# Three evictions of the steady unit in another order on ScalarE: a cross-network kernel bound by TensorE

## The chip, the cores and the metric

The kernel runs on one core of one Trainium2 chip. The metric is device time in microseconds, the median over several executions. Before the change it was 2277.09 us (three runs, 2276.94 to 2277.36).

## The reference, cut to what matters

```python
B, Din, L = 16384, 1024, 6          # bf16
x = x0
for l in range(L):
    proj = einsum('bd,de->be', x, ws[l]) + bs[l]
    x = x0 * proj + x
```

Six layers, each a 16384 x 1024 by 1024 x 1024 product, a bias, a product with x0 and a sum.

## The kernel before

The batch is cut into 16 blocks of 1024 rows. A block in one layer is a **unit**; there are 96. In a unit the product is done with seven half-size products in place of eight (P1 to P7, sums and differences of the operands are made by VectorE as T1 to T4, those of the weights are stored ahead). Two of the seven, 5 and 2, are cut once more in the same way into seven **inner products** (5p1 to 5p7, 2p1 to 2p7). So TensorE does 20 groups of four 512-wide matmuls and 14 groups of four 256-wide ones a unit.

Partial sums live in eight PSUM banks, A0 to A3 and X0 to X3. ScalarE empties them. It does three kinds of work: evictions with the bias (E1.m, E3.m, E7.m, E4.m), evictions of inner results (5e_..., 2e_...: c11, c12 and c21 are quadrants of the result, u3 an intermediate sum), and **forks** (5f1, 5f2, 2f1, 2f2, F.m): copies of a partial sum from one bank to another, so that two sums can go on from it. Each fork and eviction frees or fills a bank that a following matmul group waits for.

The order of all work is not written as a loop. Each operation has a rank, a planned time in us within the unit, and the program is emitted in order of rank as far as dependencies allow. Every engine then does its own list strictly in that order. One table, R2, is used by 87 units: all but the first eight, which have tables of their own, and the last.

```python
R2 = ranks("""
P1.0@0 P1.2@0.86 5p5@1.73 5p1@2.16 P1.3@2.6 2p1@3.46 5p2@3.9 5p6@4.34 2p5@4.78 P1.1@5.21 5p7@6.08 5p3@6.51 2p2@6.95
2p6@7.39 5p4@7.82 P6.0@8.26 P6.1@9.13 2p7@9.99 2p3@10.43 P3.0@10.86 2p4@11.73 P6.2@12.16 P3.1@13.03 P6.3@13.89
P3.2@14.75 P3.3@15.62 P7.1@16.48 ...
E1.0@1.07 5e_p5@2.38 5f1@3.03 E1.2@3.48 5e_c11@4.55 5f2@5.2 2e_p5@5.65 2f1@6.3 5e_u3@6.75 E1.3@7.23 E1.1@7.8
2e_c11@8.37 5e_c21@8.85 2f2@9.33 F.0@9.78 5e_c12@10.23 2e_u3@10.71 2e_c12@11.18 F.1@11.66 E3.0@12.11 2e_c21@12.68
F.2@13.23 E3.1@14.1 F.3@14.96 E3.2@15.82 E3.3@16.69 ...
T1@-1.14 5t13@0.59 5t2@3.06 2t13@3.39 5t4@5.13 2t2@6.6 T2@6.93 2t4@8.07 T4@8.4 5cc@10.88 T3@11.48 2cc@12.61 Q1@13.35
Qm@14.62 Qa@15.89 Ua@17.43 ...
""")
```

The inner products and their evictions (X is "5" with banks a, b = 0, 1, or "2" with banks 2, 3):

```python
inner(5, b, True)
copy(X + "e_p5", ip5[X][:], v3(b), ...)
inner(1, a, True)
copy(X + "f1", pX[b][:], pX[a][:], ...)      # first fork: bank a into bank b
inner(2, b, False)
copy(X + "e_c11", c(0, 0), v3(b), ...)
inner(6, a, False)
copy(X + "f2", pX[b][:], pX[a][:], ...)      # second fork
inner(3, b, False)
copy(X + "e_c12", iu[X][:, 0], v3(b), ...)
inner(7, a, False)                           # 2p7: bank X2 must have been forked
copy(X + "e_u3", iu[X][:, 1], v3(a), ...)
inner(4, a, False)                           # 2p4: bank X2 must have been read
copy(X + "e_c21", c(1, 0), v3(a), ...)
ttop(X + "cc", ...)                          # VectorE: needs c12, u3 and p5
...
for m in range(KH):                          # after the inner products
    xb = m if one else m % 2                 # steady units fork into X0 and X1
    group(f"P6.{m}", "6", pA[m], ...)        # P6.1 needs A1 evicted by E1.1; P6.0 needs T2
    copy(f"F.{m}", pX[xb][:], pA[m][:], ...)
    group(f"P3.{m}", "3", pX[xb], ...)
    biased(f"E3.{m}", U[:, m, :], pX[xb][:], ...)
```

Of the kernel before, what the change touches and what calls it, by code (L numbers as in the profile page):

```python
# [26 lines left out]
P1.0@0 P1.2@0.86 5p5@1.73 5p1@2.16 P1.3@2.6 2p1@3.46 5p2@3.9 5p6@4.34 2p5@4.78 P1.1@5.21 5p7@6.08 5p3@6.51 2p2@6.95  # L27
2p6@7.39 5p4@7.82 P6.0@8.26 P6.1@9.13 2p7@9.99 2p3@10.43 P3.0@10.86 2p4@11.73 P6.2@12.16 P3.1@13.03 P6.3@13.89
P3.2@14.75 P3.3@15.62 P7.1@16.48 P7.0@17.34 P7.2@18.21 P7.3@19.07 P4.1@19.93 P4.0@20.8 P4.2@21.66 P4.3@22.52
E1.0@1.07 5e_p5@2.38 5f1@3.03 E1.2@3.48 5e_c11@4.55 5f2@5.2 2e_p5@5.65 2f1@6.3 5e_u3@6.75 E1.3@7.23 E1.1@7.8  # L30
2e_c11@8.37 5e_c21@8.85 2f2@9.33 F.0@9.78 5e_c12@10.23 2e_u3@10.71 2e_c12@11.18 F.1@11.66 E3.0@12.11 2e_c21@12.68
F.2@13.23 E3.1@14.1 F.3@14.96 E3.2@15.82 E3.3@16.69 E7.0@18.41 E7.1@18.98 E7.2@19.55 E7.3@20.14 E4.0@21.87 E4.1@22.44
E4.2@23.01 E4.3@23.59
T1@-1.14 5t13@0.59 5t2@3.06 2t13@3.39 5t4@5.13 2t2@6.6 T2@6.93 2t4@8.07 T4@8.4 5cc@10.88 T3@11.48 2cc@12.61 Q1@13.35
Qm@14.62 Qa@15.89 Ua@17.43 Um@18.7 Ux@19.97 Va@21.11 Wma@23.38 Wmb@24.58 Wx@25.31 Vm@27.38 Vx@28.85
# [609 lines left out]
```

## Time and profile before

| | before |
|---|---|
| time, median | 2277.09 us |
| span of the profiled run | 2275.3 us |
| steady unit, from 2p7 to 2p7, median | 23.451 us |
| stall of TensorE ahead of 2p7, median | 0.065 us in 81 of 87 units (0.089 in three more) |
| stall of TensorE ahead of P3.3, median | 0.012 us in all 87 units |
| VectorE busy / ScalarE busy | 92% / 81% |

The stalls are read from the trace instruction by instruction: a 512-wide matmul is followed by the next start after 0.216 us, a 256-wide one after 0.109 us, and what goes beyond that is a stall; stalls of 0.003 us and more are counted. The list of waits counts otherwise: its entry of 84 waits and 15.4 us, in the prediction, holds the idle time of weight loads, and 0.118 us of each (0.216 less the 0.098 that a load takes) is the ordinary pause between two loads. 84 x (0.118 + 0.065) is 15.4. The busy share of TensorE is of no use for this, since the recorded matmuls overlap and cover gaps of this size. The lines themselves stand in the prediction.

### The profile page before, as it was taken

What the parts mean: (1) busy time and instruction counts of PE and PEld (TensorE: products, weight loads), DVE (VectorE), ACT (ScalarE), POOL (GpSimd) and SP (SyncE); (2) the same over time, 40 slices, a digit from 0 to 9 for tenths busy, and PEclk for the clock granted to TensorE, in tenths of its full rate; (3) what the DMA queues carried; (4) which work ended last, traced back from release to release, by engine and by line L of the source; (5) the groups of instructions that cost most, each with busy time, mean ns of one, the idle gap of its engine ahead of it and who ended that gap; (6) DMA issues with size and microseconds to landing.
All of it is one profiled execution on the core that took longest, in us unless ns stands there. A gap on an engine that the chain in (4) does not pass through costs nothing.

```text
span 2275.3 us, 35076 instructions
## 1 busy us (share of the span) xinstructions
PE 2267.7 (100%) x12993; PEld 1266.7 (56%) x12993; DVE 2084.0 (92%) x2331; ACT 1844.5 (81%) x3234; POOL 24.5 (1%) x46
## 2 busy tenths in 40 slices
PE   9999999999999999999999999999999999999998
PEld 4455555555555555555555555555555555555554
DVE  8999999999999999999999999999999999989997
ACT  6678888888888888888888888888888888888887
POOL 1110000000000000000000000000000000000000
PEclk9999999999999999999999999999999999999999
DMA  8779797796977969779697796977969689696872
GB/s 280 231 269 297 252 249 262 221 297 210 246 264 222 286 216 255 257 220 286 213 269 247 227 283 205 283 235 227 286 200 286 232 230 286 196 291 227 234 248 66
DMA packets 620493, 557.03 MB, mean 245 GB/s; under 512 B 391456, under 2 KB 546592, under 8 KB 620320
## 3 DMA queue, kind: packets, MB, share of 16 engines
q1 hardware_dynamic: 614240, 534.58, 79.0%
q0 software_dynamic: 5488, 19.93, 2.3%
q8 instruction: 102, 1.67, 0.3%
q14 instruction: 71, 0.58, 0.1%
q10 hardware_dynamic: 592, 0.27, 0.0%
HBM read 437.79 MB, written 52.43 MB: 215 GB/s over the span
## 4 chain that ended last, share of the span: by engine, by line
PE 99%; DMA 0%; ACT 0%; DVE 0%; issue 0%
PE pA L289 58%; PE pX L411 24%; PE pX L289 17%; DMA ev<-in_x_dram 0%; PE pX L359 0%; PE pA L505 0%; PE pX L505 0%; DVE x0T L516 0%; ACT x0T L363 0%; ACT pX L294 0%; PE pA L366 0%
## 5 line engine op out<-in xcount | busy, mean ns | idle before, releaser
L289 PEld LDWEIGHTS <-wp 128*128 128x128 bf16 x7904 | 772.5, 98 | 839.5 <-issue 1.6
L289 PE MATMUL pA<-T,wp 128*128 128x512 bf16 x4608 | 1055.1, 379 | 0.0
L298 ACT ACTIVATE ev<-pA,b_all 128x512 bf16<-128x512 f32 x1123 | 705.0, 691 | 211.2 <-PE pA L289 210.8
L411 PEld LDWEIGHTS <-wp 128*128 128x128 bf16 x4984 | 487.0, 98 | 157.3 <-issue 15.4
L202 DVE TENSOR_TENSOR ev<-ev,x0T 128x2048 bf16<-128x2048 bf16 (+2 forms) x483 | 482.9, 1002 | 8.1 <-ACT ev L298 1.5
L202 DVE TENSOR_TENSOR xst<-ev,xst 128x2048 bf16<-128x2048 bf16 x319 | 389.1, 1220 | 19.1 <-DVE ev L202 0.9
L411 PE MATMUL pX<-ti,wp 128*128 128x256 bf16 x2848 | 397.6, 272 | 0.0
L202 DVE TENSOR_TENSOR ev<-ev,ev 128x2048 bf16<-128x2048 bf16 (+1 forms) x283 | 343.9, 1215 | 25.7 <-ACT ev L298 7.6
L289 PE MATMUL pX<-xst,wp 128*128 128x512 bf16 x1376 | 336.3, 379 | 0.0
L298 ACT ACTIVATE ev<-pX,b_all 128x512 bf16<-128x512 f32 x412 | 289.4, 706 | 56.1 <-PE pX L289 46.5
L289 PE MATMUL pA<-xst,wp 128*128 128x512 bf16 x1280 | 313.5, 379 | 0.0
L294 ACT COPY pX<-pA 128x512 f32<-128x512 f32 x412 | 256.2, 625 | 39.1 <-PE pA L289 38.4
L294 ACT CAST ev<-pX 128x512 bf16<-128x512 f32 x384 | 225.2, 620 | 47.8 <-ACT ev L298 37.3
L202 DVE TENSOR_TENSOR ev<-iu,ip 128x1024 bf16<-128x1024 bf16 x178 | 122.6, 689 | 121.1 <-ACT iu L294 121.1
L294 ACT COPY pX<-pX 128x512 f32<-128x512 f32 x356 | 208.7, 587 | 8.7 <-ACT ev L294 0.2
L294 ACT CAST iu<-pX 128x512 bf16<-128x512 f32 x356 | 197.0, 640 | 0.0
L202 DVE TENSOR_TENSOR T<-xst 128x2048 bf16<-128x2048 bf16 x160 | 194.9, 1218 | 0.3
L202 DVE TENSOR_TENSOR T<-xst,T 128x2048 bf16<-128x2048 bf16 x160 | 195.0, 1219 | 0.2
L411 PE MATMUL pX<-T,wp 128*128 128x256 bf16 x1068 | 160.2, 273 | 0.0
L294 ACT CAST ip<-pX 128x512 bf16<-128x512 f32 x178 | 104.8, 589 | 54.0 <-PE pX L411 54.0
L411 PE MATMUL pX<-xst,wp 128*128 128x256 bf16 x888 | 133.2, 273 | 0.0
L202 DVE TENSOR_TENSOR xst<-ev,x0T 128x2048 bf16<-128x2048 bf16 x64 | 78.3, 1223 | 1.6
(50 smaller groups left out, 641.0 us busy)
## 6 DMA issues: line engine op xcount, KB each, us to landing
wp<-Lc SPq DMA_DIRECT2D x538, 512.0 KB, 4.6
wp<-in_ws_dram SPq DMA_DIRECT2D x287, 512.0 KB, 5.4
out_dram<-x0T SPq DMA_DIRECT2D x30, 1024.0 KB, 8.7
Lc<-wp POOLq DMA_DIRECT2D x24, 512.0 KB, 5.9
Lc<-isum POOLq DMA_DIRECT2D x12, 512.0 KB, 6.7
w<-in_ws_dram SPq DMA_DIRECT2D x5, 512.0 KB, 6.3
ev<-in_x_dram SPq DMA_DIRECT2D x3, 512.0 KB, 7.0
out_dram<-x0T SPq DMA_DIRECT2D x3, 256.0 KB, 3.9
```

The costliest lines, as they stand in the source:

```text
L202: nc.vector.tensor_tensor(out=o, in0=a, in1=b, op=op)
L289: nc.tensor.matmul(bank[:], lhsT=wt[(u, w)][:, k, m * P:(m + 1) * P], rhs=rhs[:, k, :], start=(start and k == 0), stop=(k == KH - 1), skip ...
L294: add(name, lambda: nc.scalar.copy(out=dst, in_=src), rd, wr)
L298: add(name, lambda: nc.scalar.activation(out=dst, in_=src, func=IDENT, bias=b_all[:, c:c + 1], scale=1.0), rd, wr)
L411: nc.tensor.matmul(pX[bank][:, m * NQ:(m + 1) * NQ], lhsT=wv[:, k, m * P:(m + 1) * P], rhs=rhs[:, k, :], start=(start and m == 0 and k == ...
```

## The change

Its intent is to get the second fork of inner product 2 (2f2) done earlier, so that 2p7 finds its bank ready. To make room, 2e_c11, which frees the bank that 2f2 writes, goes ahead of the eviction of bank A1 (E1.1), 5e_c21 goes behind the fork, and 2e_c21 goes ahead of E3.0. Only ranks change, and only ScalarE's list comes out different; the lists of TensorE, VectorE, GpSimd and SyncE are the same.

```diff
-E1.0@1.07 ... 5e_u3@6.75 E1.3@7.23 E1.1@7.8
-2e_c11@8.37 5e_c21@8.85 2f2@9.33 F.0@9.78 5e_c12@10.23 2e_u3@10.71 2e_c12@11.18 F.1@11.66 E3.0@12.11 2e_c21@12.68
-F.2@13.23 E3.1@14.1 ...
+E1.0@1.07 ... 5e_u3@6.75 E1.3@7.23 2e_c11@7.8 E1.1@8.28
+2f2@8.85 5e_c21@9.33 F.0@9.81 5e_c12@10.43 2e_u3@10.9 2e_c12@11.38 F.1@11.86 2e_c21@12.37 E3.0@12.85
+F.2@13.45 E3.1@14.1 ...
```

(Cuts marked with "...".)

More of the change, by code (lines that the diff above doesn't have):

```diff
@@ L29 @@
 P3.2@14.75 P3.3@15.62 P7.1@16.48 P7.0@17.34 P7.2@18.21 P7.3@19.07 P4.1@19.93 P4.0@20.8 P4.2@21.66 P4.3@22.52
-E1.0@1.07 5e_p5@2.38 5f1@3.03 E1.2@3.48 5e_c11@4.55 5f2@5.2 2e_p5@5.65 2f1@6.3 5e_u3@6.75 E1.3@7.23 E1.1@7.8
-2e_c11@8.37 5e_c21@8.85 2f2@9.33 F.0@9.78 5e_c12@10.23 2e_u3@10.71 2e_c12@11.18 F.1@11.66 E3.0@12.11 2e_c21@12.68
-F.2@13.23 E3.1@14.1 F.3@14.96 E3.2@15.82 E3.3@16.69 E7.0@18.41 E7.1@18.98 E7.2@19.55 E7.3@20.14 E4.0@21.87 E4.1@22.44
+E1.0@1.07 5e_p5@2.38 5f1@3.03 E1.2@3.48 5e_c11@4.55 5f2@5.2 2e_p5@5.65 2f1@6.3 5e_u3@6.75 E1.3@7.23 2e_c11@7.8 E1.1@8.28
+2f2@8.85 5e_c21@9.33 F.0@9.81 5e_c12@10.43 2e_u3@10.9 2e_c12@11.38 F.1@11.86 2e_c21@12.37 E3.0@12.85
+F.2@13.45 E3.1@14.1 F.3@14.96 E3.2@15.82 E3.3@16.69 E7.0@18.41 E7.1@18.98 E7.2@19.55 E7.3@20.14 E4.0@21.87 E4.1@22.44
 E4.2@23.01 E4.3@23.59
```

## The prediction

> **What bounds the kernel now.** I read the page's busy shares first, then the list of waits for TensorE and its weight loads, then the chain of work in the middle of the run, then the timelines of TensorE and ScalarE around the one place where the chain is not regular. The page says TensorE is busy all the time:
>
> ```profile
> PE 2267.7 (100%) x12993; PEld 1266.7 (56%) x12993; DVE 2084.0 (92%) x2331; ACT 1844.5 (81%) x3234; POOL 24.5 (1%) x46
> ```
>
> That alone does not say that nothing is lost, because the recorded matmuls overlap. The list of waits has one TensorE entry that repeats (total us, times, longest), and it is on the weight loads of L411, the line of the seven inner products:
>
> ```profile
> PEld L411 <- issue: 15.4, 84, 0.2
> ```
>
> 84 is nearly the number of units that use the changed order: 16 pairs of column blocks times 6 layers are 96 units, less the first eight, which have their own lists, and the last, so 87. The chain of work in one of them (start, us, what) shows the spot:
>
> ```profile
> 1000.97 0.87 PE pX L411 x8
> ...
> 1007.50 1.73 PE pA L289 x8
> 1009.23 0.94 PE pX L411 x8
> 1010.16 0.86 PE pX L289 x4
> 1011.03 0.44 PE pX L411 x4
> ...
> 1024.42 0.87 PE pX L411 x8
> ```
>
> Eight 256-wide matmuls take 0.87 us at 1000.97 and 0.94 at 1009.23. The unit's period is 1024.42 - 1000.97 = 23.45 us. The TensorE timeline of that spot (start, us) shows where the 0.07 is:
>
> ```profile
> 1008.85 0.38 PE L289 MATMUL pA<-T,wp 128*128 128x512 bf16 x1
> 1009.13 0.27 PE L411 MATMUL pX<-ti,wp 128*128 128x256 bf16 x1
> ```
>
> Starts are 0.28 apart, where 512-wide matmuls otherwise start 0.216 apart (1.73/8). So TensorE stands still 0.065 us once a unit. The matmul that waits is the first of 2p7, inner product 7 of sub-product 2. It accumulates in bank X2, which ScalarE must first have copied into X3 (the second fork, 2f2). ScalarE's timeline of the same stretch:
>
> ```profile
> 1005.87 0.59 ACT L294 CAST iu<-pX 128x512 bf16<-128x512 f32 x1
> 1006.35 1.28 ACT L298 ACTIVATE ev<-pA,b_all 128x512 bf16<-128x512 f32 x2
> 1007.50 1.09 ACT L294 CAST ev<-pX 128x512 bf16<-128x512 f32 x2
> 1008.44 0.64 ACT L294 COPY pX<-pX 128x512 f32<-128x512 f32 x1
> 1008.96 0.61 ACT L294 COPY pX<-pA 128x512 f32<-128x512 f32 x1
> 1009.43 1.62 ACT L294 CAST iu<-pX 128x512 bf16<-128x512 f32 x3
> 1010.86 0.68 ACT L294 COPY pX<-pA 128x512 f32<-128x512 f32 x1
> 1011.38 0.77 ACT L298 ACTIVATE ev<-pX,b_all 128x512 bf16<-128x512 f32 x1
> ```
>
> In order: 5e_u3; E1.3 and E1.1 (the evictions of banks A3, A1); 2e_c11 and 5e_c21; 2f2; F.0; 5e_c12, 2e_u3, 2e_c12; F.1; E3.0. The COPY at 1008.44 is 2f2. It ends at 1008.44 + 0.64 = 1009.08, and 2p7 starts 0.05 later. It has waited for no input: no idle time stands on any of these lines. ScalarE is simply late here, in a run of back-to-back evictions. **So TensorE bounds the kernel, with one ScalarE-made stall of 0.065 us in each steady unit, about 84 x 0.065 = 5.5 us in all.** That is all there is to win in this place.
>
> **What the Trainium skill says.** "PSUM — Partial Sum Buffer", section "PSUM bank collisions raise a hardware error", asks that banks be guarded by semaphores as a whole; the trace agrees in that 2p7 starts only 0.05 us after the last reader of its bank. "PSUM — Partial Sum Buffer", section "Engine vs sequencer instructions", calls ScalarE's queue strict FIFO: order alone decides when 2f2 runs, which is why a reordering can help. "TensorE: Matmul & The Clock Gate", section "Wait — 56ns, not 53.3ns?", gives N/2.4 GHz + 2.5 ns from start to start, 216 ns at N = 512; the trace has 0.216. "ScalarE: Activation LUTs", section "What ACT_TABLE_LOAD costs", has an ACTIVATE with a bias pointer at 280 + 0.833 N, 707 ns at 512, against 0.69 in an undisturbed line of this trace, and plain ones cheaper by 93; the trace's casts take 0.59.
>
> **The change part by part.** No instruction is added or removed. The comparison of the two built programs has TensorE, VectorE, GpSimd and SyncE the same, and 3237 ScalarE rows in both, in another order. Before: E1.3, E1.1, 2e_c11, 5e_c21, 2f2, F.0, 5e_c12, 2e_u3, 2e_c12, F.1, E3.0, 2e_c21, F.2. After: E1.3, 2e_c11, E1.1, 2f2, 5e_c21, F.0, 5e_c12, 2e_u3, 2e_c12, F.1, 2e_c21, E3.0, F.2. So 2f2 passes one cast, E1.1 falls behind one cast, 5e_c21 behind the fork, E3.0 behind 2e_c21.
>
> I replay this with steps from one end to the next, read from the lines above. 5e_u3 ends at 1005.87 + 0.59 = 1006.46 and the two ACTIVATEs at 1006.35 + 1.28 = 1007.63: 0.585 each. The two casts end at 1008.59: 0.48 each. Copies and casts then step 0.49; a cast right after a copy into PSUM 0.51. A ScalarE instruction that must wait for the end of the one just before it starts 0.03 later and takes its whole 0.57 (seen at every first fork, for instance 1005.39 after 2e_p5). TensorE follows ScalarE by 0.05. TensorE's slots after 2p7 come 0.065 earlier than before if the stall goes, 2p7 itself then at 1009.07.
>
> - E1.3 ends at 1007.05, 2e_c11 (its input 2p2 is done by 1006.63) at 1007.53, E1.1 at 1008.115. P6.1 needs A1 and can start at 1008.165; its slot is 1007.34 + 0.86 = 1008.20. Margin **0.04**.
> - 2f2 ends at 1008.60; 2p7 could start at 1008.65, slot 1009.07. Margin 0.42: the stall goes.
> - 5e_c21 ends at 1009.11. F.0 overwrites X0, which 5e_c21 has just read, so it now has to wait for that: start 1009.14, end 1009.71. P3.0 could start at 1009.76, slot 1010.00 - 0.065 = 1009.935. Margin 0.17.
> - 5e_c12 ends at 1010.22, 2e_u3 at 1010.71. 2p4 could start at 1010.76, slot 1010.87 - 0.065 = 1010.80. Margin **0.045**.
> - 2e_c12 ends at 1011.20, F.1 at 1011.69 (P3.1's slot 1012.10), 2e_c21 at 1012.20, E3.0 at 1012.78. F.2, again behind the reader of its bank, runs 1012.81 to 1013.38, P3.2's slot is 1013.83. E3.1 ends at 1013.99, so F.3 could start at 1014.02, but its input P6.3 holds it until 1014.15 - 0.065 = 1014.08. Margin **0.07**; from there on ScalarE waits for TensorE as before.
>
> VectorE gets 5e_c12 0.14 us later (1010.22 for 1010.08), so its run of 5cc, T3, 2cc starts later, but Q1, which before waited for 2e_c21 to end at 1012.63, now has that by 1012.20. By its own steps Q1 moves from 1012.66 to 1012.72, and its three steps (1.26, 1.26 and 1.14 us, from VectorE's timeline) would let Ua start at 1016.38. Ua waits for the last E3 anyway, until 1016.55 before and 1016.485 now, so the delay is soaked up there.
>
> **Sum.** Removed: 0.065 us in 84 units, 5.5 us. Added on ScalarE: two dependent starts a unit, some 0.1 us, in a stretch whose slack takes them. Added on TensorE: nothing if the three small margins hold. 2277.1 - 5.5 = 2271.6 us. The period of a unit goes from 23.45 to 23.385, and I find one loss of 0.01 us a unit left, at P3.3 behind F.3, which TensorE's own order makes.
>
> **The rivals.** (1) *The wait moves to P6.1*, because E1.1 now comes one cast later. Against it: 0.04 us of margin, and ScalarE's steps repeat to some 0.005 us across units. For it: margins of that size hang on the assumed step of an ACTIVATE behind a cast. If each is missed by 0.03, 87 x 0.03 = 2.6 us is given back: 2274. (2) *The wait moves to 2p4*, since F.0 and all behind it slip by 0.14 us (2e_u3 from 1010.56 to 1010.71) while TensorE comes earlier. Missed by 0.03 it costs the same: 2274. Both would leave hardly a gain: 2276. (3) *ScalarE or VectorE becomes the bound*. ScalarE still has about 1 us of idle time twice a unit, ahead of the E7 and E4 evictions (1.04 and 1.03 in its timeline). VectorE has less: 0.1 us ahead of Ua. Were that missed, 2p1's operand, VectorE's last result of a unit, would come later, but that is 0.25 us early now (its add ends at 1002.25, 2p1 starts at 1002.54). (4) *DMA*: busy some 80%, weights by ring; no TensorE wait for it in steady units, and a period shorter by 0.3% changes little.
>
> **Range and chances.** About 75% for the full gain (2271 to 2272.3), 15% for a part of it through rivals 1 or 2, the rest for none or worse. Runs of the kernel before differ by 0.4 us. I say 2271.8, with 2270.8 to 2274.0. No outcome comes near 2% (45 us): even a stall of 0.3 us in each unit would add only 26 us.
>
> **What would show it.** Right: the entry of 84 waits at the weight loads of L411 is gone; the chain shows 0.87 instead of 0.94 for the eight matmuls that begin with 2p7; a unit takes 23.385 us; ScalarE's copy 2f2 starts 1.6 us after E1.3's start, not 2.1, and F.0 shows a gap of 0.03 behind a ScalarE cast. VectorE's idle time ahead of 5cc grows from 1.38 us by some 0.14. Wrong: a wait of TensorE at P6.1 (banks A, L289) or at 2p4 (X2, L411) in each steady unit, or Ua on VectorE released by its own predecessor and not by ScalarE.

## The result, and the profile after

The changed kernel took **2272.19 us** (median of six runs, 2271.97 to 2272.44); the kernel before took 2277.23 us (six runs, 2276.71 to 2277.75). The ratio is 0.9978, with a 95% interval of 0.9965 to 0.9991. (A ratio here is the mean time of one kernel's fast runs over that of the other's in the same rounds, so not quite the ratio of the medians.) That is 5.0 us or 0.22% faster, within 2%.

The waits of the changed kernel (us in total, times, longest) have this left of the entry with 84 waits:

```profile
PEld L411 <- issue: 0.5, 2, 0.3
```

The chain of work in a steady unit of the changed kernel (start, us, what):

```profile
999.14 0.87 PE pX L411 x8
...
1005.67 0.21 PE pA L289
1005.89 0.05 issue
1005.94 1.46 PE pA L289 x6
1007.40 0.87 PE pX L411 x8
1008.27 0.86 PE pX L289 x4
```

The eight matmuls that begin with 2p7 now take 0.87 us, as such a group does elsewhere. The line "issue" is no stall. This trace lacks 239 matmul records: the page counts 12754 matmuls beside 12993 weight loads, where the trace before had 12993 of each. Where the record of a 512-wide matmul is missing, two starts mostly stand 0.430 to 0.432 us apart, two steps of 0.215 or 0.216. So the page's TensorE share of 99% after 100% says nothing either, and in this document starts are compared only where no record is missing.

ScalarE's timeline of the same stretch:

```profile
1004.52 0.70 ACT L298 ACTIVATE ev<-pA,b_all 128x512 bf16<-128x512 f32 x1
1005.10 0.60 ACT L294 CAST ev<-pX 128x512 bf16<-128x512 f32 x1
1005.57 0.72 ACT L298 ACTIVATE ev<-pA,b_all 128x512 bf16<-128x512 f32 x1
1006.15 0.63 ACT L294 COPY pX<-pX 128x512 f32<-128x512 f32 x1
1006.66 0.63 ACT L294 CAST ev<-pX 128x512 bf16<-128x512 f32 x1
1007.32 0.57 ACT L294 COPY pX<-pA 128x512 f32<-128x512 f32 x1
1007.80 1.57 ACT L294 CAST iu<-pX 128x512 bf16<-128x512 f32 x3
```

In order: E1.3, 2e_c11, E1.1, 2f2, 5e_c21, F.0, then the three casts. The fork 2f2 starts 1.63 us after E1.3 and ends at 1006.78; 2p7 starts at 1007.24, 0.46 us later instead of 0.05. F.0 starts 0.03 us behind 5e_c21, whose bank it overwrites.

Taking the trace from the first steady 2p7 to the last (86 unit lengths) gives the account of the gain:

| | before | changed |
|---|---|---|
| 86 units, us | 2017.33 | 2012.73 |
| median unit, us | 23.451 | 23.390 |
| excess of the units over 86 medians, us | 0.55 | 1.19 |
| stalls ahead of 2p7 | 84, median 0.065 | none |
| stalls ahead of P6.0 | 3 long ones | 52, median 0.005, and 3 long ones |
| stalls ahead of 2p1 | none | 2, of 0.13 and 0.15 |
| stalls ahead of P3.3 | 87, median 0.012 | 87, median 0.012 |

86 x 0.061 = 5.2 us came from the regular units, and 0.64 us of it was lost again in a few irregular ones. Another 0.4 us lies ahead of the first and behind the last of these units. The first steady unit's own stall at 2p7, 0.09 us, is part of that; the rest can't be told from noise, since these two ends together differ by 0.4 us between two traces of the changed kernel (this one and e9_changed_again). Something new stands at P6.0. P6.0 needs T2 from VectorE. VectorE's T2 and the first matmul of P6.0 (start, us) before:

```profile
677.62 1.22 DVE L202 TENSOR_TENSOR T<-xst,T 128x2048 bf16<-128x2048 bf16 x1
...
678.92 0.38 PE L289 MATMUL pA<-T,wp 128*128 128x512 bf16 x1
```

and after:

```profile
653.27 1.22 DVE L202 TENSOR_TENSOR T<-xst,T 128x2048 bf16<-128x2048 bf16 x1
...
654.54 0.38 PE L289 MATMUL pA<-T,wp 128*128 128x512 bf16 x1
```

Before, T2 ended at 678.84, some 0.08 us ahead of P6.0, and no stall stood there. After, P6.0 starts 0.05 us behind T2's end, and it does so in most units (0.052 to 0.056 in 66 of the 87): that is the latency of a wait that binds. VectorE has come up to TensorE.

### The profile page after: what moved, and what is told of

Its sections match the earlier page's. It is cut to its first block, busy times and chain, and to the rows that moved or that the text cites. A ratio compares the mean times of both kernels' runs of the same rounds, so it can differ in the third digit from the quotient of the medians.

```text
span 2270.3 us, 34837 instructions
## 1 busy us (share of the span) xinstructions
PE 2250.3 (99%) x12754; PEld 1266.9 (56%) x12993; DVE 2077.3 (91%) x2331; ACT 1855.9 (82%) x3234; POOL 24.5 (1%) x46
## 4 chain that ended last, share of the span: by engine, by line
PE 97%; DVE 2%; issue 1%; ACT 0%; DMA 0%; DVEq 0%; ACTq 0%
PE pA L289 57%; PE pX L411 23%; PE pX L289 17%; DVE ev L202 1%; DVE xst L202 1%; DVE T L202 0%; DVE ti L202 0%; DMA ev<-in_x_dram 0%; ACT pX L294 0%; PE pX L359 0%; ACT iu L294 0%; ACT ev L294 0%; PE pA L505 0%; ACT ev L298 0%; PE pX L505 0%
## 5 line engine op out<-in xcount | busy, mean ns | idle before, releaser
L298 ACT ACTIVATE ev<-pA,b_all 128x512 bf16<-128x512 f32 x1123 | 717.5, 692 | 211.1 <-PE pA L289 163.8
L298 ACT ACTIVATE ev<-pX,b_all 128x512 bf16<-128x512 f32 x412 | 285.8, 697 | 46.0 <-PE pX L289 45.2
L289 PE MATMUL pA<-xst,wp 128*128 128x512 bf16 x1205 | 302.4, 379 | 3.9
L294 ACT CAST ev<-pX 128x512 bf16<-128x512 f32 x384 | 232.1, 606 | 48.0 <-ACT ev L298 37.6
L294 ACT COPY pX<-pA 128x512 f32<-128x512 f32 x412 | 239.2, 583 | 32.9 <-PE pA L289 19.1
```

What stands on the lines that cost most here:

```text
L289: nc.tensor.matmul(bank[:], lhsT=wt[(u, w)][:, k, m * P:(m + 1) * P], rhs=rhs[:, k, :], start=(start and k == 0), stop=(k == KH - 1), skip ...
L294: add(name, lambda: nc.scalar.copy(out=dst, in_=src), rd, wr)
L298: add(name, lambda: nc.scalar.activation(out=dst, in_=src, func=IDENT, bias=b_all[:, c:c + 1], scale=1.0), rd, wr)
```

## The experiments

The theory: (a) the whole gain is the stall at 2p7; (b) moving the fork alone is not enough, because what follows it on ScalarE is late for other waiters, so the other moves are needed to keep 2p4 and VectorE in time; (c) what is left at P6.0, little in regular units and more in irregular ones, comes from VectorE's run of work after 5cc having lost its slack. The rivals: the other moves are idle or carry the gain themselves; the margin at P6.1 is not real; what is left is TensorE's own.

Ten kernels ran, in three groups on one chip each, all correct. The ten compare with the kernel before in the same group:

| run | what | median us | before, same group | regular stalls in the trace (median x count) |
|---|---|---|---|---|
| e1_fork_only | before + fork ahead of 5e_c21 | 2277.09 | 2276.74 | P6.0: 0.058 x 65; 2p4: 0.056 x 16 |
| e2_swap_only | before + 2e_c11 ahead of E1.1 | 2276.86 | 2276.74 | 2p7: 0.064 x 84 |
| e3_c21_back | changed, 2e_c21 behind E3.0 | 2273.16 | 2276.74 | P6.0: 0.010 x 59 |
| e7_a1_last | changed, E1.1 behind the fork | 2321.99 | 2276.74 | P6.1: 0.582 x 87 |
| e9_changed_again | the changed kernel | 2272.65 | 2277.52 | P6.0: 0.005 x 48 |
| e4_t3_early | changed + T3 ahead of 5cc | 2271.53 | 2277.52 | none (P6.0: one of 0.186) |
| e6_four_banks | e4 + forks into four banks | 2270.81 | 2277.52 | none |
| e8_fork_only_t3_early | e1 + T3 ahead of 5cc | 2277.31 | 2277.52 | P6.0: 0.058 x 65; 2p4: 0.055 x 16 |
| e10_all_but_swap | e8 + 2e_c21 ahead of E3.0 | 2276.30 | 2277.21 | 2p4: 0.049 x 86 |
| e5_before_t3_early | before + T3 ahead of 5cc | 2277.09 | 2277.21 | 2p7: 0.065 x 84 |

All but e7_a1_last have five runs; that one had a single look. Every kernel but e6_four_banks also has the 0.012 us at P3.3. Single long stalls are left out of the table, and so are stalls at 2p4 in e1 and e8 that are under 0.01. Runs of one kernel differ by some 0.4 to 1.9 us, so differences of half a microsecond are read from the stalls in the traces and not from the medians.

### e1_fork_only: the fork alone

```diff
-2e_c11@8.37 5e_c21@8.85 2f2@9.33 F.0@9.78
+2e_c11@8.37 2f2@8.85 5e_c21@9.33 F.0@9.78
```

> The kernel before with one of the three moves: the second fork 2f2 passes 5e_c21, E1.1 stays ahead of 2e_c11. My theory (the gain is the stall at 2p7, and the other moves only keep other banks in time): 2f2 now stands right behind the cast of its own bank and starts 0.03 us behind it, ends 1008.71 in the unit that the prediction replays, so 2p7 no longer waits; but everything behind is 0.10 us later than in the changed kernel, 2e_u3 ends at 1010.80 and 2p4 may start at 1010.855 instead of in its slot at 1010.80. So a stall of about 0.055 us a unit comes back, at 2p4 or, if VectorE's later start makes T2 late, at P6.0: unit 23.44 us, time about 2276.4. Rival (the fork's move alone is the gain, the other moves are idle): 2272.2.

Measured: 2277.09 us, ratio 1.0001 (0.9988 to 1.0013). The stall at 2p7 is gone and a stall of 0.058 us stands at P6.0. In the second layer's units, one in six, T2 is early; there P6.0 does not wait, and 2p4 stalls by 0.056 us. The same two lines for this kernel, T2 and P6.0:

```profile
700.96 1.22 DVE L202 TENSOR_TENSOR T<-xst,T 128x2048 bf16<-128x2048 bf16 x1
...
702.23 0.38 PE L289 MATMUL pA<-T,wp 128*128 128x512 bf16 x1
```

P6.0 again starts 0.05 us behind T2. A wait has taken the place of the one removed, of nearly the same size. The rival that the fork's move alone is the gain falls. The expectation named both places and the size of the stall; the total is 0.7 us above it, in part in the irregular units (an excess of 1.05 us against 0.55 before).

### e2_swap_only: the swap of 2e_c11 and E1.1 alone

```diff
-E1.3@7.23 E1.1@7.8 2e_c11@8.37 5e_c21@8.85
+E1.3@7.23 2e_c11@7.8 E1.1@8.37 5e_c21@8.85
```

> The kernel before with only 2e_c11 put ahead of E1.1 (eviction of bank A1); 2f2 stays behind 5e_c21. My theory: 2f2 still ends at about 1009.08, so 2p7 stalls by 0.065 us in 84 units as before, and P6.1 does not wait although E1.1 ends 0.49 us later (margin 0.04): 2277.2, within 0.4 of the kernel before. Rival (the swap itself saves something, or P6.1 waits): 2272 to 2275, or 2279 and more with a TensorE wait at P6.1.

Measured: 2276.86 us, ratio 1.0000. The stall at 2p7 is there in 84 units as before, and no stall at P6.1. So the swap saves nothing by itself and its cost, a later E1.1, fits into P6.1's margin.

### e7_a1_last: how much margin P6.1 has

```diff
-2e_c11@7.8 E1.1@8.28 2f2@8.85 5e_c21@9.33
+2e_c11@7.8 2f2@8.28 E1.1@8.85 5e_c21@9.33
```

> The changed kernel with E1.1 put behind 2f2 as well, that is one place further back. My theory (P6.1 has only 0.04 us of margin behind E1.1): 2f2 starts 0.03 us behind 2e_c11 and ends at 1008.13, E1.1 at 1008.73, so P6.1, whose slot is 1008.20, starts at 1008.78: a stall of 0.58 us in each of 87 units, 2271.7 + 50 = about 2322, all of it at P6.1. Rival (TensorE finds room, or its weight loads hide it): under 2285.

Measured: 2321.99 us, one look. TensorE stalls 0.582 us ahead of P6.1 in all 87 units. The waits of this kernel:

```profile
PEld L289 <- issue: 61.7, 90, 0.7
```

The expected size was 0.58 us and 2322 us. So ScalarE's list could be replayed here to some 0.01 us from its steps and dependencies, and E1.1 stands as far back as it may: one place further costs 2%.

### e3_c21_back: the third move undone

```diff
-F.1@11.86 2e_c21@12.37 E3.0@12.85
+F.1@11.86 E3.0@12.37 2e_c21@12.85
```

> The changed kernel with 2e_c21 put back behind E3.0. My theory (this third move does nothing for TensorE): E3.0 ends 0.5 us earlier, 2e_c21 at 1012.76 and not 1012.20, so Q1 on VectorE waits for 2e_c21 again instead of for 2cc, by about 0.01 us: 2272.2 to 2272.8. Rival (moving 2e_c21 out of F.2's way carries part of the gain): 2274 or more, with TensorE waits at P3.2.

Measured: 2273.16 us, ratio 0.9984 (0.9971 to 0.9998), a little above the expected 2272.2 to 2272.8. In the trace the stall at P6.0 rises from 0.005 to 0.010 us and the unit from 23.390 to 23.393, which is 0.3 us in all; no stall stands at P3.2. The rest of the difference to 2272.19 lies in the traces ahead of the first and behind the last steady unit, where two traces of the changed kernel itself also differ by 0.4 us. So in the changed kernel this move is worth only some tenths of a microsecond.

This run also closes the square of fork and swap. It has both and gains (ratio 0.9984); e1 has the fork alone (1.0001), e2 the swap alone (1.0000), and neither gains anything. The fork and the swap together make the gain.

### e9_changed_again, e4_t3_early: VectorE relieved

```diff
-T4@8.4 5cc@10.88 T3@11.48 2cc@12.61
+T4@8.4 T3@9.6 5cc@10.88 2cc@12.61
```

VectorE waits some 1.5 us ahead of 5cc for a ScalarE result. T3, a difference of two inputs that have long been there, takes 1.2 us and stood behind 5cc.

> The changed kernel itself, as the yardstick of this group: 2272.2 within 0.5, with short TensorE waits of about 0.005 us at P6.0 in most steady units and a unit of 23.390 us.

> The changed kernel with VectorE's T3 moved from behind 5cc to ahead of it, where VectorE waits some 1.5 us for ScalarE. My theory (after the change VectorE's back-to-back run from 5cc to T2 of the next unit just reaches P6.0, and costs 0.005 us a unit and some 0.2 us in three disturbed units): the run gets 1.1 us shorter, Ua waits for the last E3 again, T2 ends some 0.075 us or more ahead of P6.0, the waits at P6.0 are gone (0.75 us in all in the trace of the changed kernel) and so are the longer ones in the disturbed units: 0.8 to 1.1 us faster than the changed kernel of this group, unit 23.385 us. Rival (the 0.005 us are TensorE's own or the weight loads'): the same time as the changed kernel.

Measured: 2272.65 us for the changed kernel in this group and 2271.53 us with T3 early, 1.1 us less. The stalls at P6.0 are gone but for one. The waits of VectorE show where its slack is now; the changed kernel first, then the one with T3 early:

```profile
DVE ev L202 <- ACT iu L294: 132.0, 89, 1.6
DVE ev L202 <- ACT ev L298: 8.7, 10, 4.2
```

```profile
DVE ev L202 <- ACT iu L294: 60.6, 176, 0.7
DVE ev L202 <- ACT ev L298: 47.0, 94, 4.2
DVE ev L202 <- ACT ev L294: 26.5, 87, 0.3
```

In the second list Ua waits for the last E3 (L298) in some 87 units. It did so before the change too, in waits too short for this list: there Ua starts 0.03 us behind the last E3. VectorE starts its last stretch on ScalarE's word again and has time to spare.

One part of the expectation was wrong. The median unit is 23.389 us and not 23.385; the changed kernel's is 23.390. The regular stalls of 0.005 us at P6.0 had cost 0.001 us a unit, some 0.1 us in all. The gain is in irregular units: their excess over the median went from 1.17 us in this group's run of the changed kernel to 0.39. In the two largest of them Qa starts 0.46 and 0.47 us behind Qm, where 0.104 is usual. The first of them in the first trace of the changed kernel (the other is at 2043.39, and the kernel before has both in the same units):

```profile
543.95 1.22 DVE L202 TENSOR_TENSOR ev<-ev,x0T 128x2048 bf16<-128x2048 bf16 x1
545.63 1.23 DVE L202 TENSOR_TENSOR xst<-ev,xst 128x2048 bf16<-128x2048 bf16 x1 [0.46 <-PE pX L289]
```

VectorE loses some 0.35 us there, and in the changed kernel TensorE loses all of it: these two units are 0.350 and 0.372 us longer than the median. 0.13 and 0.15 us of this stand ahead of 2p1, whose operand is a result of VectorE (Wx), and 0.23 ahead of P6.0. At 2p1 in the first of them:

```profile
554.69 1.23 DVE L202 TENSOR_TENSOR xst<-ev,xst 128x2048 bf16<-128x2048 bf16 x1
...
555.97 0.27 PE L411 MATMUL pX<-xst,wp 128*128 128x256 bf16 x1
```

In the kernel before, the two units are 0.092 us longer each; with T3 early TensorE feels nothing of them. Why these two steps are late isn't shown.

### e8_fork_only_t3_early and e10_all_but_swap: is the swap needed?

e8 is e1 with T3 early. e10 also has 2e_c21 ahead of E3.0, so it has all of the change but the swap, and VectorE relieved:

```diff
 (e8 against before: 2f2 ahead of 5e_c21, T3 ahead of 5cc; e10 also:)
-F.1@11.66 E3.0@12.11 2e_c21@12.68
+F.1@11.66 2e_c21@12.11 E3.0@12.68
```

> The fork alone moved (as in e1_fork_only) together with T3 early. In e1_fork_only the stall of 2p7 was gone and 0.058 us stood at P6.0 in its place, since 5cc started 0.1 us later. My theory (ScalarE's own chain is too late for 2p4 as well, VectorE only hides it): with VectorE relieved, P6.0 does not wait, and 2p4 waits about 0.06 us in each of 87 units for 2e_u3: 2276.2, so moving 2e_c11 ahead of E1.1 is a needed part of the change. Rival (VectorE alone made the stall of e1_fork_only): 2271.3, like T3 early on the changed kernel.

Measured: 2277.31 us, and the same stalls as in e1, at P6.0. The theory's place for the stall, 2p4, holds in the second layer's units alone (0.054 us); elsewhere it was missed, and so was the rival's time. The waits of VectorE say why:

```profile
DVE ev L202 <- ACT ev L294: 76.3, 87, 0.9
```

With T3 out of the way VectorE's Q1 waits 0.88 us for 2e_c21, which in e8 stands behind E3.0. So T3's place gained nothing there: VectorE's run now began at Q1, as late as before. This is where the third move of the change counts, in a kernel without the swap; with the swap and T3 early it was not undone. I therefore added it:

> All of the change but the swap of 2e_c11 and E1.1, and T3 early. In e8_fork_only_t3_early the stall stayed at P6.0 with T3 early, because Q1 on VectorE then waited 0.88 us for 2e_c21, which stood behind E3.0 as in the kernel before. Here 2e_c21 is ahead of E3.0, so VectorE is out of the way. My theory (without the swap ScalarE is 0.10 us later from 2f2 on, and 2p4 has a margin of only 0.045): 2p4 waits 0.055 to 0.06 us for 2e_u3 in each of 87 units, P6.0 does not wait: about 2276.5, and a unit of 23.44 us. Rival (2e_c21 behind E3.0 was the only cause of the stall in e1 and e8, the swap is idle): 2271.5, like T3 early on the changed kernel.

Measured: 2276.30 us, ratio 0.9996. P6.0 is free, and 2p4 stalls 0.049 us in 84 units. The chain of work of one of them:

```profile
1289.96 0.87 PE pX L411 x8
1290.84 0.86 PE pX L289 x4
1291.70 0.48 PE pX L411 x4
```

2p4's four matmuls take 0.48 us here and 0.44 elsewhere. The rival falls, and the swap is needed with VectorE relieved as well (e4 is this kernel with the swap): without it all of ScalarE behind 2f2 is 0.1 us later, because 2f2 must then wait for the end of the cast just ahead of it, and that is more than 2p4's margin. With the swap E1.1 fills that gap. The stall is 0.049 us and not the 0.055 to 0.06 that I expected.

### e5_before_t3_early: was VectorE a bound before?

The same edit of T3, on the kernel before.

> The kernel before with T3 ahead of 5cc. My theory (in the kernel before VectorE is no bound: Ua waits for the last E3, and T2 ends 0.075 us ahead of P6.0): the stall at 2p7 stays at 0.065 us in some 87 units and the time is that of the kernel before within 0.5: only the three disturbed units can gain some 0.1 us each. Rival (T3's place is worth the same in both kernels, about 1.1 us, so it has nothing to do with the change): 1.1 us faster than the kernel before.

Measured: 2277.09 us against 2277.21, ratio 1.0000 (0.9987 to 1.0014), the stalls at 2p7 unchanged, unit 23.451 us. The edit that gained 1.1 us on the changed kernel is worth nothing on the kernel before, so the rival falls. But this run does not answer the question in its heading, because the edit relieves nothing there: T2 still ends 0.078 us ahead of P6.0 in the median unit, 0.077 before. 2e_c21 stands behind E3.0, and Q1 waits for it as in e8:

```profile
DVE ev L202 <- ACT ev L294: 76.7, 87, 0.9
```

The trace of the kernel before answers it: where a wait for T2 binds, P6.0 starts 0.053 us behind it, and TensorE stalls at P6.0 in three units only. So VectorE was no bound in the regular units before, but by 0.024 us only. What a real relief of VectorE would gain on the kernel before was not tried.

### e6_four_banks: the last regular stall

```diff
-            xb = m if one else m % 2
+            xb = m
```

> T3 early as in the run before, and the forks F.2 and F.3 go into banks X2 and X3 and no longer into X0 and X1. My theory (P3.3 loses 0.012 us a unit because F.3 has to wait for two engines: for P6.3, and for the last reader of X1): F.3 starts about 0.04 us behind P6.3 and not 0.09, P3.3 no longer waits, 86 x 0.012 = 1.0 us less than the run before: about 2270.2, unit 23.373 us. Rival (the 0.012 us stay, since P6.3 comes only one group ahead of P3.3 and the fork itself takes 0.57): no difference to the run before.

Measured: 2270.81 us (2270.28 to 2271.85), ratio 0.9969 (0.9957 to 0.9982), 0.7 us less than e4. No regular stall is left; the median unit is 23.380 us, 0.009 less than e4's. With F.3 in bank X3, which was read long ago, it waits for TensorE alone. The last matmul of P6.3 and F.3, in e4 first:

```profile
1011.22 0.38 PE L289 MATMUL pA<-T,wp 128*128 128x512 bf16 x1
1011.70 0.57 ACT L294 COPY pX<-pA 128x512 f32<-128x512 f32 x1
```

and in this kernel:

```profile
1010.93 0.38 PE L289 MATMUL pA<-T,wp 128*128 128x512 bf16 x1
1011.35 0.57 ACT L294 COPY pX<-pA 128x512 f32<-128x512 f32 x1
```

F.3 starts 0.09 us behind the matmul's recorded end in e4 and 0.04 behind it here. The rival, that P6.3 comes too shortly ahead, falls. The expected 0.012 us a unit was too much by 0.003. This version is the fastest of all that ran, 6.7 us below the kernel before in its group by the medians.

## Why the prediction was right

- **"TensorE bounds the kernel, with one ScalarE-made stall of 0.065 us in each steady unit"**: right. The stall is gone in the changed kernel, and the shorter regular units make up 5.2 us. e2 shows that without the fork's move nothing happens.
- **"5.5 us" (the sum)**: measured 5.0. Two terms were mis-sized. First, a stall of 0.065 us was counted in full, but the unit became only 0.061 us shorter in the changed kernel and would be 0.062 with no stall left at P6.0 (e4: 23.389). In the trace before, the four starts that follow the stalled one come 0.1084 us apart on the mean, in e4 0.1092: TensorE wins back some 0.003 us. e6 shows the same: a stall of 0.012 removed, 0.009 gained. That is 0.3 us of 5.5. Second, the irregular units, which the prediction took as given, lost 0.64 us more than before. About 0.4 us was gained outside the stretch of 86 units, within the noise of these two ends but for the first unit's 0.09.
- **ScalarE's replay with its margins 0.04 at P6.1, 0.42 at 2p7, 0.17 at P3.0, 0.045 at 2p4 and 0.07 at F.3**: no stall stands at any of these in the changed kernel. P6.1 starts 0.086 us behind the end of E1.1 and 2p4 0.089 behind that of 2e_u3, where a wait that binds takes 0.05: margins of 0.036 and 0.039. They are confirmed by what it takes to break them: e7 (0.582 us where the replay gives 0.58) and e10 (0.049 where it gives 0.055).
- **"The delay is soaked up there" (VectorE at Ua)**: wrong for five of six layers. The prediction gave Ua 0.1 us of margin. In the changed kernel Ua starts 0.06 to 0.07 us behind the end of the last E3 where a wait on it alone takes 0.03, and follows Qa without a pause: it is released by its own predecessor, which the prediction had named as a sign of being wrong. Two steps were too short. Q1 was given 0.03 us behind 2cc; it took 0.105. Qa was given 0.03 behind Qm, as in the unit that I read; that was a unit of the first layer, where Qa writes another buffer than it reads. In the other layers it took 0.104. In the trace an extra wait instruction stands ahead of these two (they wait for VectorE's own step and for another engine), and none ahead of the quick ones. The idle time ahead of 5cc grew from 1.38 to 1.52 us in the unit read, as predicted.
- **The rivals**: (1) and (2), a wait at P6.1 or 2p4, did not come. (3), VectorE as the bound, came at P6.0 in regular units, at a price of some 0.1 us. At 2p1's operand, where the prediction looked for it, it came in two units alone. The prediction took that operand (Wx) for VectorE's last result of a unit; Vx comes later on VectorE's list, and T2, which P6.0 waits for, needs it. What it costs is protection: the irregular steps of VectorE now reach TensorE, the two largest in full. (4), DMA, shows no wait of TensorE in the regular units of any trace.
- **The range**, 2270.8 to 2274.0 around 2271.8, held the 2272.2. The sum did not owe that to luck, but VectorE's part did: Ua is 0.035 us later than the replay has it, T2 had 0.024 us of room ahead of P6.0, and the prediction had not looked at that place. A larger error there would have come back in most units.

## What to carry to other kernels

When an in-order engine makes another wait, moving the late instruction forward moves everything behind it as well, so list every waiter of that stretch with its margin and replay the new list from measured steps. Here the fork alone gave nothing, and the swap, which is idle when tried alone, is what kept the gain; the third move was worth some tenths of a microsecond. Before a run is taken as a test of an engine's slack, check in its trace that the edit gave that engine slack: e5 did not. After a stall is removed, look for the engine that has lost its slack, and fill its own waiting time with work that depends on nothing, as T3 ahead of 5cc did.

## What the Trainium skill lacked or had wrong

- "TensorE: Matmul & The Clock Gate", section "Back-to-back issue gap", puts the sustained spacing in a stream of weight loads and matmuls at about 131 ns for N = 512 and says that N/2.4 + 2.5 over-counts there. In these traces every group of four 512-wide matmuls with their weight loads takes 0.86 us, 216 ns each, through whole units without a stall; 256-wide ones take 109.
- "Perfetto Trace Analysis", section "Identifying Dependency Chains", says that a wait on several engines may be put into an extra instruction, but not what it costs. Here VectorE pauses 0.034 us behind its own predecessor with one wait and 0.104 with two, and the fork F.3 starts 0.09 us behind its matmul with two waits where single ones start 0.04 behind.
- I found no page with the latency of a hand-over between engines. ScalarE's end to TensorE's start took 0.050 to 0.052 us, VectorE's end to TensorE's start 0.052 to 0.056, and ScalarE behind its own predecessor 0.03.
- I found no page that says that a stall of TensorE is partly won back: 0.065 us cost 0.062, and 0.012 cost 0.009.
- I found no page that says how missing matmul records look in a trace: 239 of 12993 are missing in the trace of the changed kernel, at the same places, every 50 to 61 matmuls, in four other traces. They show up as gaps of one step and lower the busy share.
